# Moving a large SBUF buffer by 384 bytes: a DMA-bound two-pass kernel with its rows 128 bytes past, or on, a multiple of 256

## The chip, the cores and the metric

The kernel runs on one core of a Trainium2 chip. The metric is device time in microseconds (us), the median over several executions. All executions compared below are in the fast state, but for one experiment that was run once and has no state. Ratios are the mean time of one kernel's fast runs over the mean time of the other's fast runs of the same rounds, so they are not quite the ratio of the medians quoted. Readings of packets and spans come from one profiled execution of each kernel, and that one need not lie at the median.

Two words are used throughout. A **packet** is one record of the DMA trace: a contiguous run of bytes that one of the 16 DMA engines moves, with a start, a duration and a size. A start **on 256** is an address that is a multiple of 256 B; one **off 256** is not.

## The reference, cut to what matters

```python
H = W = 384; C = 384                     # x: (1, 384, 384, 384) bf16, 113 MB
g = jnp.einsum("bhwc->bc", x) / (H * W)  # mean of each channel over all pixels
s = _sigmoid(g * w1d[0])                 # k = 1, so the convolution is a product
return x * s[:, None, None, :]           # scale every pixel's channels
```

Every element is needed twice, once for the mean and once for the scaling, and of the 1152 rows that x has in each partition the kernel's buffer in SBUF takes 275. The kernel keeps part of x there (some of it packed, as several fields of bits share words) and reads the rest again: 190 MB are read, of an x of 113.

## The kernel before

All large data lies in one tile, the arena, of 275 rows of C = 384 bf16 values. A row of 384 values is 768 B = 3 x 256 B, so the place of the arena fixes where every row starts relative to 256.

```python
arena = pool.tile([P, ROWS, C], bf16, name="arena")      # ROWS = 275: 211200 B in each partition
ones = pool.tile([P, P], bf16, name="ones")
s_bf = pool.tile([P, C], bf16, name="s_bf")
w_bf = pool.tile([1, 1], bf16, name="w_bf")
...                                                      # zeros, w_sc, seen, worst, odd, odd_i
```

Tiles are placed in the order of these lines, at steps of 32 B. Loads and stores take whole rows of the arena, so that each of the 128 partitions gives one contiguous run on both sides:

```python
def view(t, r0, n):                                      # n rows in each partition, contiguous in HBM
    return t[r0 * P : (r0 + n) * P, :].rearrange("(p r) c -> p r c", r=n)
...
nc.sync.dma_start(out=arena[:, a : a + hi - lo, :], in_=view(xf, r0, n)[:, lo:hi, :])   # load
...
nc.sync.dma_start(out=view(of, r0, n)[:, lo:hi, :], in_=arena[:, a : a + hi - lo, :])   # store
```

Pass one loads everything; TensorE sums rows into PSUM (L226), VectorE and ScalarE pack and check some of them (L250, L256, L290). Pass two scales on VectorE (L432) and stores, and loads again what was not kept. One queue issues all 138 transfers.

Of the kernel before, what the change touches and what calls it, by code (L numbers as in the profile page):

```python
# [127 lines left out]
def kernel(  # L128
# [12 lines left out]
    P = nc.NUM_PARTITIONS  # L141
    B, H, W, C = x.shape
# [5 lines left out]
    bf16, f32, u16, u32 = x.dtype, mybir.dt.float32, mybir.dt.uint16, mybir.dt.uint32  # L148
# [14 lines left out]
    ROWS = base  # L163
# [7 lines left out]
    pool = ctx.enter_context(tc.tile_pool(name="sb", bufs=1))  # L171
    psum = ctx.enter_context(tc.tile_pool(name="psum", bufs=1, space=bass.MemoryType.PSUM))

    pieces = [(g, lo, min(PIECE, q - lo)) for g, q in enumerate(QS) for lo in range(0, q, PIECE)]
    arena = pool.tile([P, ROWS, C], bf16, name="arena")
    ones = pool.tile([P, P], bf16, name="ones")
    s_bf = pool.tile([P, C], bf16, name="s_bf")
    w_bf = pool.tile([1, 1], bf16, name="w_bf")
    zeros = pool.tile([P, P], bf16, name="zeros")
    w_sc = pool.tile([P, 1], f32, name="w_sc")  # L180
    seen = pool.tile([P, 2 * len(pieces)], f32, name="seen")
    worst = pool.tile([P, 1], f32, name="worst")
    odd = pool.tile([P, 1], bf16, name="odd")
    odd_i = pool.tile([P, 1], mybir.dt.int32, name="odd_i")
    bank0 = psum.tile([P, nc.PSUM_BANK_SIZE_BYTES // 4], f32, name="bank0")
    acc, votes = bank0[:, 0:C], bank0[:, C : C + 1]
# [564 lines left out]
```

## Time and profile before

| | before |
|---|---|
| time | 728.79 us, median of 3 (726.57 to 729.08); the profiled execution took 729.99 |
| bytes moved | 303.67 MB by the main queue: 190 MB read from HBM, 113 MB written |
| transfers | 82 loads, 56 stores, 128 data packets each |
| busiest | DMA 98.4%, VectorE 68% |

Two lines of the list of DMA issues (transfers of one size, KB each, median us from issue to landing) and one of the groups by form (busy us, mean ns, idle before):

```profile
arena<-in_x_dram SPq DMA_DIRECT2D x17, 4608.0 KB, 34.8
out_dram<-arena SPq DMA_DIRECT2D x6, 4608.0 KB, 44.4
...
L432 DVE TENSOR_TENSOR arena<-arena,s_bf 128x6144 bf16<-128x6144 bf16 x26 | 85.7, 3351 | 48.2 <-DMA arena<-in_x_dram 48.2
```

4608 KB at the 430 GB/s of the stretches below take 11 us; they land 35 to 44 us after issue, in a queue that is busy for 98.4% of the span, so I take it that others are ahead of them. VectorE's scaling waits for the loads (48.2 us in this group). The prediction below shows the other lines.

### The profile page before, as it was taken

How to read it: one execution, taken by the hardware profiler on the slowest of the kernel's cores; microseconds unless marked ns; L12 is line 12 of the kernel's file. 1: busy time of each engine (PE TensorE's matmuls, PEld its weight loads, DVE VectorE, ACT ScalarE, POOL GpSimd, SP SyncE). 2: the span in 40 equal slices, each digit the busy share in tenths (PEclk: the TensorE clock that was granted, in tenths of full speed). 3: DMA queues.
4: the chain of work that ended last, by engine and by line, in shares of the span. 5: the costliest groups of instructions: out<-in, count | busy, mean ns of one | idle time of the engine just before them, and what ended most of it. 6: DMA issues, size and time to landing. Idle time of an engine off the chain costs nothing.

```text
span 728.2 us, 3243 instructions
## 1 busy us (share of the span) xinstructions
PE 211.9 (29%) x1202; PEld 118.1 (16%) x1202; DVE 496.2 (68%) x469; ACT 115.4 (16%) x92; POOL 0.2 (0%) x4
## 2 busy tenths in 40 slices
PE   4677978889887770000000000000000000000000
PEld 2334535545443430000000000000000000000000
DVE  4600007887985729998999997999969993355330
ACT  3600005665764520001000000000000000000000
POOL 0000000000000000000000000000000000000000
PEclk9899999999999996555555555555555555555555
DMA  9999999999999978999999999999999999999996
GB/s 379 426 433 436 425 419 429 430 430 427 426 422 424 409 315 334 415 420 428 431 415 442 421 428 426 427 442 430 417 425 438 434 434 427 421 433 448 419 430 273
DMA packets 19890, 303.87 MB, mean 417 GB/s; under 512 B 2210, under 2 KB 2210, under 8 KB 6434
## 3 DMA queue, kind: packets, MB, share of 16 engines
q1 hardware_dynamic: 19872, 303.67, 98.4%
q8 instruction: 9, 0.15, 0.1%
q14 instruction: 7, 0.06, 0.0%
q10 hardware_dynamic: 2, 0.00, 0.0%
HBM read 190.41 MB, written 113.25 MB: 417 GB/s over the span
## 4 chain that ended last, share of the span: by engine, by line
DMA 56%; DVE 27%; PE 6%; another core or an unknown queue 4%; ACT 2%; SPq 1%; issue 0%; DVEq 0%
DMA arena<-in_x_dram 41%; DVE arena L432 18%; DMA out_dram<-arena 16%; PE bank L226 6%; DVE arena L250 5%; DVE arena L256 4%; ACT arena L290 2%; SPq L220 1%; ACT s_bf L423 0%; PE bank L504 0%; DVE odd L499 0%; DVE odd_i L508 0%; DVE worst L494 0%; DVEq L112 0%
## 5 line engine op out<-in xcount | busy, mean ns | idle before, releaser
L432 DVE TENSOR_TENSOR arena<-arena,s_bf 128x1536 bf16<-128x1536 bf16 (+8 forms) x102 | 241.8, 2411 | 74.9 <-DMA arena<-in_x_dram 60.8
L250 DVE TENSOR_SCALAR arena<-arena 128x1536 uint16<-128x1536 uint16 (+2 forms) x247 | 145.8, 633 | 116.5 <-DMA arena<-in_x_dram 104.1
L226 PE MATMUL bank<-arena,ones 128*128 128x384 bf16 x1152 | 203.7, 338 | 57.8 <-DMA arena<-in_x_dram 57.8
L226 PEld LDWEIGHTS bank<-arena,ones 128*128 128x128 bf16 x1152 | 113.2, 101 | 148.0 <-DMA arena<-in_x_dram 63.8
L256 DVE TENSOR_TENSOR arena<-arena 128x1536 uint16<-128x1536 uint16 (+2 forms) x114 | 121.0, 1061 | 8.5 <-PE bank L226 6.4
L290 ACT ACTIVATE arena<-arena 128x3072 uint16<-128x3072 uint16 (+1 forms) x38 | 102.5, 2696 | 147.8 <-DVE arena L250 147.8
L360 ACT COPY arena<-bank 128x512 uint32<-128x512 uint32 (+1 forms) x7 | 4.0, 570 | 70.7 <-DMA out_dram<-arena 70.6
L241 PE MATMUL bank<-ones,zeros 128*128 128x384 bf16 x48 | 8.3, 326 | 0.0
L290 ACT ACTIVATION_READ_ACCUMULATOR arena<-arena 128x1 f32 x38 | 7.1, 186 | 0.0
L241 PEld LDWEIGHTS bank<-ones,zeros 128*128 128x128 bf16 x48 | 4.7, 98 | 3.1
L504 PE MATMUL bank<-odd,ones 128*128 128x1 bf16 x1 | 0.2, 186 | 15.8 <-DVE odd L499 15.8
L360 ACT COPY bank<-arena 128x512 uint32<-128x512 uint32 (+1 forms) x7 | 3.6, 566 | 0.0
L504 PEld LDWEIGHTS bank<-odd,ones 128*128 128x128 bf16 x1 | 0.1, 104 | 16.2 <-DVE odd L499 16.2
L423 ACT ACTIVATE s_bf<-bank,w_sc 128x384 bf16<-128x384 f32 x1 | 0.6, 580 | 12.6 <-PE bank L226 12.6
L719 ACT ACT_TABLE_LOAD x1 | 1.3, 1283 | 0.7 <-PEq L735 0.7
L320 DVE TENSOR_SCALAR w_sc<-bank 128x1 f32<-128x1 f32 x1 | 0.2, 159 | 1.4 <-PE bank L315 1.4
L315 PE MATMUL bank<-w_bf,ones 1*128 1x1 bf16 x1 | 0.2, 182 | 2.4 <-DMA w_bf<-in_w1d_dram 2.4
L310 DVE MEMSET ones<- 128x128 bf16 x1 | 0.2, 165 | 1.0 <-SPq L106 1.0
L315 PEld LDWEIGHTS bank<-w_bf,ones 1*128 1x128 bf16 x1 | 0.1, 100 | 2.4 <-DMA w_bf<-in_w1d_dram 2.4
L508 DVE CAST odd_i<-bank 128x1 int32<-128x1 f32 x1 | 0.2, 159 | 0.3 <-PE bank L504 0.3
L494 DVE TENSOR_REDUCE worst<-seen 128x1 f32<-128x38 f32 x1 | 0.2, 182 | 0.0
L499 DVE TENSOR_SCALAR odd<-worst 128x1 bf16<-128x1 f32 x1 | 0.2, 156 | 0.0
(5 smaller groups left out, 0.5 us busy)
## 6 DMA issues: line engine op xcount, KB each, us to landing
arena<-in_x_dram SPq DMA_DIRECT2D x17, 4608.0 KB, 34.8
out_dram<-arena SPq DMA_DIRECT2D x6, 4608.0 KB, 44.4
arena<-in_x_dram SPq DMA_DIRECT2D x21, 1248.0 KB, 11.7
arena<-in_x_dram SPq DMA_DIRECT2D x9, 2304.0 KB, 27.5
out_dram<-arena SPq DMA_DIRECT2D x8, 2304.0 KB, 29.4
arena<-in_x_dram SPq DMA_DIRECT2D x4, 4512.0 KB, 34.8
out_dram<-arena SPq DMA_DIRECT2D x3, 4512.0 KB, 27.0
out_dram<-arena SPq DMA_DIRECT2D x9, 1248.0 KB, 12.1
```

The costliest lines, as they stand in the source:

```text
L220: lambda: nc.sync.dma_start(out=arena[:, a : a + hi - lo, :], in_=view(xf, r0, n)[:, lo:hi, :]),
L226: return nc.tensor.matmul(acc, lhsT=ones[:], rhs=arena[:, i, :], start=first, stop=last)
L241: lambda: nc.tensor.matmul(acc, lhsT=zeros[:], rhs=ones[:, None, :].to_broadcast([P, C // P, P]), start=False, stop=False),
L250: lambda: nc.vector.tensor_scalar(out=dst, in0=src, scalar1=s0, scalar2=s1, op0=op0, op1=op1),
L256: "DVE", lambda: nc.vector.tensor_tensor(out=dst, in0=a, in1=b, op=op), reads=reads, writes=writes
L290: lambda: nc.scalar.activation(out=y, in_=y, func=ACTF.Copy, accum_out=seen[:, 2 * k + i : 2 * k + i + 1]),
L315: lambda: nc.tensor.matmul(votes, lhsT=ones[0:1, :], rhs=w_bf[0:1, 0:1], start=True, stop=True),
L360: "ACT", lambda: nc.scalar.copy(dst.bitcast(u32), src.bitcast(u32)), reads=reads, writes=writes
L423: lambda: nc.scalar.activation(out=s_bf[:], in_=acc, func=ACTF.Sigmoid, scale=w_sc[:, 0:1]),
L432: lambda: nc.vector.tensor_tensor(out=v, in0=v, in1=s_bf[:, None, :].to_broadcast([P, n, C]), op=Op.mult),
L504: lambda: nc.tensor.matmul(votes, lhsT=ones[:], rhs=odd[:], start=True, stop=True),
L719: nc.scalar.preload_act_table(ACTF.Sigmoid)
```

## The change

The intent is that every row in SBUF starts on 256. Five small tiles go ahead of the arena; they take up 384 B. Nothing else is touched.

```diff
-    arena = pool.tile([P, ROWS, C], bf16, name="arena")
+
     ones = pool.tile([P, P], bf16, name="ones")
-    s_bf = pool.tile([P, C], bf16, name="s_bf")
     w_bf = pool.tile([1, 1], bf16, name="w_bf")
-    zeros = pool.tile([P, P], bf16, name="zeros")
     w_sc = pool.tile([P, 1], f32, name="w_sc")
-    seen = pool.tile([P, 2 * len(pieces)], f32, name="seen")
     worst = pool.tile([P, 1], f32, name="worst")
     odd = pool.tile([P, 1], bf16, name="odd")
+    arena = pool.tile([P, ROWS, C], bf16, name="arena")
+    s_bf = pool.tile([P, C], bf16, name="s_bf")
+    zeros = pool.tile([P, P], bf16, name="zeros")
+    seen = pool.tile([P, 2 * len(pieces)], f32, name="seen")
     odd_i = pool.tile([P, 1], mybir.dt.int32, name="odd_i")
```

## The prediction

> **What bounds the kernel now.** I read the activity slices of the page first, then its queue table, then the busy time by stretches, then the waits, then the single packet records of the trace. The slices and queues:
>
> ```profile
> DVE  4600007887985729998999997999969993355330
> DMA  9999999999999978999999999999999999999996
> GB/s 379 426 433 436 425 419 429 430 430 427 426 422 424 409 315 334 415 420 428 431 415 442 421 428 426 427 442 430 417 425 438 434 434 427 421 433 448 419 430 273
> DMA packets 19890, 303.87 MB, mean 417 GB/s; under 512 B 2210, under 2 KB 2210, under 8 KB 6434
> ...
> q1 hardware_dynamic: 19872, 303.67, 98.4%
> ```
>
> The DMA row is at 9 nearly everywhere; the exceptions are slices 15 and 16 (255 to 291 us, where the column sum ends, the sigmoid runs and the first rows are scaled) and the last one. Queue 1 keeps the 16 DMA engines busy 98.4% of the span, so any gain has to come out of the engine time of the transfers or out of the small remainder. The stretches say how fast the engines go while they are busy, and which engine would be next:
>
> ```profile
> core 0: us, PE busy (x) PEld busy (x) DVE busy (x) ACT busy (x) POOL busy (x), PEclk, DMA share, GB/s
> ...
> 60.00:120.00 60.00, 49.38 (x280) 28.12 (x280) 6.78 (x10) 4.95 (x3) 0.00 (x0) 0.94 1.00 430
> ...
> 272.00:300.00 28.00, 0.19 (x1) 0.10 (x1) 27.03 (x24) 0.55 (x1) 0.00 (x0) 0.59 0.89 349
> 300.00:400.00 100.00, 0.00 (x0) 0.00 (x0) 95.73 (x87) 3.99 (x7) 0.00 (x0) 0.50 1.01 425
> 400.00:500.00 100.00, 0.00 (x0) 0.00 (x0) 94.70 (x73) 0.00 (x0) 0.00 (x0) 0.50 1.01 429
> ...
> 600.00:700.00 100.00, 0.00 (x0) 0.00 (x0) 46.65 (x16) 0.00 (x0) 0.00 (x0) 0.50 1.00 430
> 700.00:728.20 28.20, 0.00 (x0) 0.00 (x0) 0.00 (x0) 0.00 (x0) 0.00 (x0) 0.50 0.76 327
> ```
>
> With the DMA share at 1.00 the kernel moves 425 to 430 GB/s, whether it only loads (60 to 120 us) or loads and stores (400 to 700 us). VectorE is the second limit: 94.70 of 100 us busy between 400 and 500, so about 5% of room there, more elsewhere. Last, the waits:
>
> ```profile
> DVE arena L250 <- DMA arena<-in_x_dram: 104.1, 12, 78.2
> ...
> PEld bank L226 <- DMA arena<-in_x_dram: 63.8, 35, 7.3
> DVE arena L432 <- DMA arena<-in_x_dram: 60.8, 9, 20.4
> PE bank L226 <- DMA arena<-in_x_dram: 57.8, 36, 7.5
> ```
>
> PE and VectorE wait for loads; the DMA seldom waits for them. The bound is the engine time of the packets.
>
> Each of the 138 transfers that queue 1 makes (82 loads, 56 stores) shows as 128 data packets, one for each partition and as long as that transfer's rows in it, and 16 packets of 4 B that report the end: 138 x 144 = 19872, the count in the table. The records give a duration for each packet. Most common values, in ns, beside the bytes at 27.2 B/ns (the slope between 4608 B and 36864 B: 32256 B in 1186 ns):
>
> ```
> bytes   count  most common  bytes/27.2  over
>  3072     512      121        112.9      8.1
>  9984    3840      375        367.1      7.9
> 18432    2176      686        677.6      8.4
> 36864    2944     1364       1355.3      8.7
>     4    2208        9          0.1      8.9
> ```
>
> So a data packet costs its bytes at 27.2 B/ns, plus about 8.3 ns, whatever its size. Loads alone (before 260 us) and stores alone (after 700 us) have the same commonest value: 1364 ns for 36864 B in both. Per engine the span is made of: 303.67 MB / 16 / 27.2 = 697.8 us of bytes; 17664 / 16 = 1104 data packets x 8.3 ns = 9.2 us; 138 reports x 9 ns = 1.2 us; some 8.3 us by which packets ran longer than that rule (716.4 us of packet time in all, less the three sums); and 728.2 - 716.4 = 11.8 us idle (2.0 us before the first packet, 2.2 us after the last, most of the rest around 270 to 280 us).
>
> [...]
>
> **The change part by part.** The built program places the arena at byte 16512 of each partition before, 64 x 256 + 128, and at 16896 = 66 x 256 after. A row of 384 bf16 values has 768 B = 3 x 256, so before every row starts 128 B past a boundary of 256 and after every row starts on one. Nothing is added or removed: on every engine the two programs have the same instructions in the same order (PE 12 merged rows in both, VectorE 303, ScalarE 24, GpSimd 69, the issuing queue 116), apart from shifted line numbers. Semaphores and buffers stay.
>
> - DMA, per byte: nothing to gain. [...]
> - Longer packets: some of the 8.3 us could go if the offset causes them. They lie mostly where loads run alone and near 272 to 300 us, and rarely in the mixed stretch, at the same offset. I count 0 to 1 us.
> - VectorE: the scaling takes 3351 ns for 6144 elements and 1749 for 3072, 1.92 elements per ns; the bit operations 960 ns for 3072 and 554 for 1536, 3.78 per ns. One is half the other per element, and both grow linearly in size, so I see no per-row penalty to remove. 0 us. PE reads rows in 326 ns at the minimum, which is also its median, and waits for loads; 0 us.
> - What passes to the end: the DMA is the bound in most stretches and VectorE has 4 to 5% of room in the tightest, so a saving of 0.7% in engine time passes nearly whole.
>
> The sum is 0 if the 8.3 ns are a fixed price, 2.1 us if only reads pay, 5.2 us if both sides do: at most 0.7% of 728.8, far inside 2%.
>
> **The rivals.**
> First, no effect: the time stays at 728 to 729 us. For it: loads and stores cost the same 8.3 ns, though in a load it is memory that is read, in rows that are whole multiples of 768 B, and in a store it is SBUF. A rule for reads alone would make the two differ, unless something else fills the gap. And the 4 B reports, which [...]have nothing to do with the arena, last 9 ns[...]. Both speak for a price per packet that knows nothing of alignment.[...] I give it 65%.
> Second, both sides pay: about 723.5 us. For it: equal cost of loads and stores[...]. Against: the reports. 20%.
> Third, reads alone pay: 726.5 us. Against it: the equal cost. 10%.
> Fourth, the last 5%: the move changes something unseen, such as the longer packets of the first 260 us, where a better placement might give 2 to 4 us more; or VectorE, fed a little faster between 300 and 600 us, takes the bound and part of a DMA gain is lost[...].[...]
>
> **Range and chances.** The weighted mean is 0.65 x 728.5 + 0.20 x 723.5 + 0.10 x 726.5 + 0.05 x 726 = 727.2; as the most likely case lies above it, I say 727.5. The three runs of before spread from 726.6 to 729.1 already, so the upper end is 730 and the lower end 722.5, just under the second rival. Faster by over 2% means under 714.2 us, 14.6 us to be saved: more than the whole price of the packets, 9.2 us. I give it 0.02. Slower by over 2% needs 14.6 us of new work where none is added: 0.01.
>
> **What would show it right or wrong.** In the packet records: 36864 B still at 1364 ns in loads and in stores (no effect)[...]. The queue's share of busy time should stay near 98.4% and the stretch from 600 to 700 us at 430 GB/s, against 431 to 432 if packets shrink. Packet counts, the 138 transfers and the VectorE durations should not change. The prediction is wrong if [...]the time per byte changes, if 18432 B loads lose their scatter above 686 ns, or if VectorE's 3351 ns moves.

Where the marks stand, passages are cut that rest on a price per packet which no trace or run of this case shows: how the fixed 8.3 ns might be made up, why nothing was to be gained per byte, the terms of the sum for stores and for loads, part of the case for the first two rivals, and some of the signs to look for. The sum came to 0 us if the 8.3 ns are a fixed price, 2.1 us if only reads pay and 5.2 us (0.7% of the time) if both sides do. The terms behind the 2.1 and 5.2 us are those cut, and the rivals at 726.5 and 723.5 us and the low end of the range stand on them; what is left of the sum is 0 per byte, for VectorE and for PE, and 0 to 1 us for longer packets.

## The result, and the profile after

The changed kernel takes **722.32 us** (median of 4, 721.76 to 722.96), the kernel before beside it 728.62 us (median of 4). The ratio is 0.9919, with a 95% interval of 0.9898 to 0.994. That is 0.8% faster: clear of noise, and inside 2%.

The page of the changed kernel, the lines that answer to those of before (lines of the source are one higher, L432 is now L433):

```profile
span 721.2 us, 3243 instructions
...
DMA  9999999999999988999999999999999999999997
GB/s 386 426 429 430 444 414 428 432 431 430 427 428 426 418 342 320 408 424 430 432 430 439 424 436 432 427 446 428 428 433 431 441 431 435 422 439 428 438 436 323
DMA packets 19890, 303.87 MB, mean 421 GB/s; under 512 B 2210, under 2 KB 2210, under 8 KB 6434
...
q1 hardware_dynamic: 19872, 303.67, 98.7%
```

The same packets and bytes went 7.0 us sooner (span 728.2 to 721.2), at 421 instead of 417 GB/s. The profiled executions (729.99 and 722.96 us) are slower than their medians, so this difference is somewhat more than the 6.3 us between the medians. The busy time by stretches:

```profile
60.00:120.00 60.00, 50.18 (x275) 28.25 (x276) 6.09 (x9) 4.22 (x3) 0.00 (x0) 0.91 1.00 431
...
300.00:400.00 100.00, 0.00 (x0) 0.00 (x0) 96.62 (x89) 4.00 (x7) 0.00 (x0) 0.50 1.01 429
400.00:500.00 100.00, 0.00 (x0) 0.00 (x0) 96.04 (x77) 0.00 (x0) 0.00 (x0) 0.50 1.01 433
...
600.00:700.00 100.00, 0.00 (x0) 0.00 (x0) 43.11 (x14) 0.00 (x0) 0.00 (x0) 0.50 1.00 433
700.00:721.20 21.20, 0.00 (x0) 0.00 (x0) 0.00 (x0) 0.00 (x0) 0.00 (x0) 0.50 0.79 342
```

The last number of a line is GB/s, the one before it the DMA share. At the same share of 1.00 to 1.01 the rate went from 425 to 429 (300 to 400 us), from 429 to 433 and from 430 to 433. VectorE (the third pair of numbers) is busy for 96.04 of 100 us, so it comes nearer to being the bound but does not become it. The compute itself is unchanged, and what waits for loads waits a little less:

```profile
L433 DVE TENSOR_TENSOR arena<-arena,s_bf 128x6144 bf16<-128x6144 bf16 x26 | 85.7, 3351 | 46.1 <-DMA arena<-in_x_dram 46.1
...
DVE arena L251 <- DMA arena<-in_x_dram: 100.8, 11, 77.8
...
DVE arena L433 <- DMA arena<-in_x_dram: 57.5, 9, 20.2
PE bank L227 <- DMA arena<-in_x_dram: 54.9, 33, 7.2
```

**Where the time came from** is in the packet records. With loads and stores taken together, the commonest duration of every size is what it was: 36864 B take 1364 ns, 18432 B 686, 9984 B 375, 4 B 9, so the price of 8.3 ns on a packet did not move. What moved are the packets that run *longer* than that. I take the excess of each packet over the commonest duration of its size, sum it, and divide by 16 for one engine:

| stretch, us | before, us per engine | after |
|---|---|---|
| 0 to 60, loads | 0.84 | 0.65 |
| 60 to 250, loads | 1.55 | 0.68 |
| 250 to 300, end of the sum, first stores | 2.51 | 2.15 |
| 300 to 700, loads and stores | 3.46 | 0.43 |
| all | 8.36 | 3.90 |

Two different things shrank. From 60 to 250 us 3836 of some 5046 packets ran up to 12 ns long before (1.18 us of the 1.55); after, 17 did. From 300 to 700 us few packets ran long, but by much: 206 by more than 50 ns before (3.36 us), 29 after (0.42 us). Given to loads and stores in the order of the program, 190 of the 206 and 27 of the 29 were loads.

The first of the two is not a price that every load packet pays. By slices of 10 us, packets at most 20 ns over the commonest exceed their bytes (at 27.2 B/ns) in the kernel before by 8.5 ns from 10 to 20 us, as after the change (8.4); by 9.5 from 30 to 40; and by about 12 only from 50 us on, where after the change it stays between 8.0 and 9.5 up to 250 us. From 300 us on, where loads and stores alternate, ordinary load packets (at most 50 ns too long) stand at 8.61 ns before and 8.24 after. The 4 ns belong to long runs of loads alone.

The end of the program shows what this does to the total. The last transfer reports its end 16 times, once for each engine. The mean of these reports moved from 722.27 to 717.70 us, 4.57 us sooner, which agrees with the 4.45 us by which the summed packet time of an engine fell (716.40 to 711.95). But the last of the 16 moved from 726.29 to 719.26, 7.03 us sooner: the engines had drifted 5.68 us apart before and 2.58 us after, and the end waits for the slowest. So 4.57 us are shorter packets on the average engine, and 7.03 - 4.57 = 2.46 us are engines that end closer together.

The second number has the same source as the first. The records can be sorted into 16 sequences, one for each engine, since each packet starts just before the one ahead of it ends (99% of them fit so), mostly by 3 to 4 ns; of the 8.2 ns on a packet some 4 to 5 then keep the engine from the next one. From 300 us on the sum by which an engine's packets exceed their bytes plus 8.2 ns each is 2.1 to 7.2 us before, with a median of 2.5, and 0.0 to 1.6 us after, with a median of 0.2. That sum and the time at which the engine ends go together (correlation 0.98 before, 0.93 after): the long packets fall mostly on a few engines, and the program ends with the one that got most of them.

### The profile page after: what moved, and what is told of

Read it like the earlier page. It is cut to its first block, busy times and chain, and to the rows that moved or that the text cites. A ratio compares the mean times of both kernels' runs of the same rounds, so it can differ in the third digit from the quotient of the medians.

```text
span 721.2 us, 3243 instructions
## 1 busy us (share of the span) xinstructions
PE 213.6 (30%) x1202; PEld 118.9 (16%) x1202; DVE 496.2 (69%) x469; ACT 115.4 (16%) x92; POOL 0.2 (0%) x4
## 4 chain that ended last, share of the span: by engine, by line
DMA 56%; DVE 27%; PE 6%; another core or an unknown queue 4%; ACT 2%; SPq 1%; issue 0%; DVEq 0%
DMA arena<-in_x_dram 41%; DVE arena L433 18%; DMA out_dram<-arena 15%; DVE arena L251 6%; PE bank L227 6%; DVE arena L257 4%; ACT arena L291 2%; SPq L221 1%; ACT s_bf L424 0%; PE bank L505 0%; DVE odd L500 0%; DVE odd_i L509 0%; DVE worst L495 0%; DVEq L112 0%
## 5 line engine op out<-in xcount | busy, mean ns | idle before, releaser
L433 DVE TENSOR_TENSOR arena<-arena,s_bf 128x1536 bf16<-128x1536 bf16 (+8 forms) x102 | 241.8, 2411 | 71.8 <-DMA arena<-in_x_dram 57.5
```

Source lines behind the costliest of these rows:

```text
L433: lambda: nc.vector.tensor_tensor(out=v, in0=v, in1=s_bf[:, None, :].to_broadcast([P, n, C]), op=Op.mult),
```

## The experiments

The theories: **A**, the start of the arena's rows relative to 256 lengthens the packets of loads, which write there. Its rivals: **B**, the small tiles' own new places; **C**, chance. Within A, the question is whether the transfers do it by themselves (A1) or only against compute (A2), which side of a transfer counts, and what the long packets from 300 us on are.

One table has the readings of all but one run. "Loads alone" is the mean time by which packets between 60 and 250 us exceed their bytes at 27.2 B/ns (those at most 20 ns over the commonest). "Long" counts packets over 50 ns too long between 300 and 700 us. "Spread" is the time between the first and last of the last transfer's 16 reports. The runs come from different chips; the kernel before had a median of 728.2 to 728.9 us.

| run | SBUF start, mod 256 | median us | loads alone, ns | long: count, us per engine | spread, us |
|---|---|---|---|---|---|
| before | 128 | 728.62 | 12.05 | 206, 3.36 | 5.68 |
| after | 0 | 722.32 | 8.26 | 29, 0.42 | 2.58 |
| rest_aligned | 128 | 729.90 | 12.08 | 147, 2.82 | 6.87 |
| arena_only | 0 | 722.96 | 8.22 | 28, 0.37 | 2.32 |
| off64 | 64 | 729.82 | 12.22 | 113, 2.41 | 5.60 |
| off32 | 32 | 730.08 | 13.22 | 148, 3.03 | 6.14 |
| dma_off128 | 128 | 721.94 | 12.11 | 106, 1.95 | 6.09 |
| dma_off0 | 0 | 715.27 | 8.22 | 15, 0.34 | 2.87 |
| dram128_sb0 | 0 | 716.57 | 8.25 | 29, 0.62 | 3.33 |
| dram128_sb128 | 128 | 720.06 | 12.19 | 28, 0.54 | 3.64 |
| l0_s0 | loads 0, stores 0 | 715.51 | 8.22 | 33, 0.61 | 4.06 |
| l0_s128 | loads 0, stores 128 | 714.26 | 8.23 | 60, 0.95 | 4.34 |
| l128_s0 | loads 128, stores 0 | 715.80 | 12.19 | 22, 0.27 | 3.41 |

### Which tile counts

**rest_aligned** leaves the arena at byte 16512, 128 off, and brings ones, s_bf and zeros onto 256:

```diff
     arena = pool.tile([P, ROWS, C], bf16, name="arena")
+    # w_bf, w_sc, worst, odd now stand here (4 x 32 B), then:
     ones = pool.tile([P, P], bf16, name="ones")
     s_bf = pool.tile([P, C], bf16, name="s_bf")
```

> Arena left 128 B past a multiple of 256 as in the kernel before, but ones, s_bf and zeros moved to multiples of 256. Theory A (the start of the arena rows, as the place that loads write to, lengthens load packets): nothing gained, 728 to 729 us; in the packet records loads before 250 us keep their scatter of 4 to 8 ns over the commonest value, and load packets over 50 ns too long stay near 250 after 300 us's neighbourhood (180 or so from 300 to 700 us). Theory B (the small tiles' own placement makes the gain): 722 to 723 us. Theory C (chance of the run or of the chip): no rule, anything from 721 to 729.

**arena_only** puts the arena at 16640 = 65 x 256, and leaves ones, s_bf and zeros 32 B off:

```diff
+    # w_bf, w_sc, worst, odd stand here (4 x 32 B), then:
     arena = pool.tile([P, ROWS, C], bf16, name="arena")
+    # then odd_i (32 B), ones, s_bf, zeros, seen
```

> Arena at a multiple of 256 (16640, another one than the change's 16896), but ones, s_bf and zeros left 32 B past one. Theory A: the whole gain, 721.5 to 723 us, few long load packets between 300 and 700 us (under 40). Theory B: none, 728 to 729 us.

Against the kernel before in the same rounds (728.42 us), rest_aligned has the ratio 1.0011 (0.9992 to 1.0029) and arena_only 0.9928 (0.9914 to 0.9942). B falls: with the small tiles moved alone nothing is gained. C falls too: two aligned layouts and two at 128 give the same two times, and nearly the same packet readings (rest_aligned has 147 long packets, where some 180 had been expected). The rates by slices of the two, rest_aligned first:

```profile
GB/s 381 424 433 436 425 420 428 429 430 428 424 425 421 410 315 333 417 427 425 431 426 441 412 434 417 439 438 434 414 433 430 427 448 415 426 435 439 429 436 255
```

```profile
GB/s 383 428 426 431 444 414 431 430 433 426 431 427 428 419 346 322 409 425 428 434 428 439 425 437 429 431 439 437 429 432 433 437 429 429 432 433 442 432 430 329
```

The last slice tells the spread: 255 GB/s where the engines end far apart, as in the kernel before (273), and 329 where they end together, as after (323).

### Transfers without compute

**dma_off128** and **dma_off0** are the kernels before and after with all compute left out. Their outputs are wrong, which doesn't matter for the times.

```diff
     def add(self, eng, emit, reads=(), writes=(), dma=False, after=()):
+        if eng != "SP":
+            return None
```

> All work of the compute engines taken out (wrong result on purpose), the transfers left, arena 128 B off as before. Some 707 to 718 us, as bytes alone are 698 us and packets' fixed price adds some 5 to 10 us. If the offset lengthens load packets by itself (A1), this is 4 to 7 us slower than the same with the arena on a multiple of 256, with scattered load packets. If it does so only against the compute engines' accesses to SBUF (A2), both take the same within 1 us and no load packet scatters.

> The same transfers alone, arena on a multiple of 256. A1: 4 to 7 us faster than with the arena 128 B off. A2: equal within 1 us.

721.94 against 715.27 us: 6.7 us, as much as in the full kernel. A1 holds and A2 falls: no compute engine is needed for the loss, and since no VectorE or TensorE instruction is left, no speed of theirs is needed for a gain of this size. Both times lie at or above the upper part of what I had expected for the bare transfers (707 to 718). Stretches of dma_off128, then of dma_off0:

```profile
60.00:250.00 190.00, 0.00 (x0) 0.00 (x0) 1.00 1.00 427
...
500.00:600.00 100.00, 0.00 (x0) 0.00 (x0) 1.00 1.00 429
```

```profile
60.00:250.00 190.00, 0.00 (x0) 0.00 (x0) 1.00 1.01 431
...
500.00:600.00 100.00, 0.00 (x0) 0.00 (x0) 1.00 1.00 432
```

With loads alone the rate is 427 against 431 GB/s, with loads and stores 429 against 432 in this stretch (400 to 500 us likewise; from 300 to 400 both have 432, from 600 to 700 it is 432 against 434).

### Other offsets

**off64** and **off32** put 192 B and 160 B of small tiles ahead of the arena, so that it starts at 16704 (64 past a multiple) and 16672 (32 past):

```diff
+    # w_bf, w_sc, worst, odd, odd_i stand here (off32), and a pad of 32 B (off64)
     arena = pool.tile([P, ROWS, C], bf16, name="arena")
```

> The full kernel with the arena 64 B past a multiple of 256. If only a start on a multiple of 256 is free (A), 727 to 731 us, with scattered load packets. If the penalty is that of 128 alone (an odd half of 256), or grows with the offset, it lies between 722.5 and 728. If a multiple of 64 were enough, 128 B would have cost nothing, so that is out already.

> The full kernel with the arena 32 B past a multiple of 256[...]. A with a penalty that does not depend on the offset: 727 to 731 us. A penalty that grows with the bytes below the start: about 724 us.

Both took the loss whole: 729.82 and 730.08 us, ratios 1.0025 (1.0011 to 1.0038) and 1.003 (1.0016 to 1.0045) to the kernel that is 128 off. An offset of 32 B costs no less than one of 128; loads alone cost it even a nanosecond more (13.22 against 12.05). So the loss does not grow with the offset among these three, and 32 or 64 is not enough of an alignment.

### Which side of a transfer

**dram128_sb0** and **dram128_sb128** are the two bare kernels again, but every transfer except that of the very first rows takes its place in HBM 128 B earlier (the store of the first rows leaves a row out, to keep off its neighbour). Where x and out start in HBM the trace does not say; "128 off" is relative to where they are in the runs without a shift. That the unshifted ones lie on 256 is not shown, so for HBM only the effect of a shift by 128 B is.

```diff
     def view(t, r0, n):
-        return t[r0 * P : (r0 + n) * P, :].rearrange("(p r) c -> p r c", r=n)
+        lo = r0 * P * C - (64 if r0 else 0)             # 64 elements = 128 B earlier
+        return (xl if t is xf else ol)[lo : lo + n * P * C].rearrange("(p r c) -> p r c", r=n, c=C)
```

> Transfers alone (wrong result on purpose), arena on a multiple of 256, but every transfer but those of the first rows reads x and writes out 128 B earlier, so the HBM side starts 128 B off. Theory D (only the start of the SBUF side of a load counts): 714.5 to 716.5 us, clean load packets, as with the arena at a multiple of 256 and nothing shifted (715.27). Theory E (source and destination must lie alike within 256): about 722 us, scattered loads. Theory F (any write off 256, to HBM too): stores' packets scatter here, over 718 us.

> The same, with the arena 128 B off as well, so both sides are off alike. D: 721 to 723 us (721.94 with the arena alone off). E: about 715 us, clean. F: slower than 722 us.

For loads alone the packets answer: reading HBM 128 off into rows on 256 costs 8.25 ns over the bytes, as unshifted (8.22), and reading it 128 off into rows that are off alike costs 12.19. Only where the load *writes* counts, and a source that lies alike does not help; for this part E falls. For stores, I took the packets between 300 and 700 us, the long ones left out: 8.23 ns over the bytes in dma_off0, 8.23 also in dma_off128, where they read SBUF 128 off, but 12.39 in dram128_sb0, where they write HBM 128 off. So it is not SBUF either, but the place of the write, at about 4 ns (12.39 less 8.23) for a packet on average; here F was right, though the time of over 718 us that it was to have did not come. By the time, dram128_sb0 is 1.3 us slower than dma_off0 (roughly). It was run at another time.

dram128_sb128 has a surprise: off on every side, it took 720.06 us, and hardly any long packets (28), while dma_off128, off in SBUF alone, has 106. No theory had that.

### What the long packets are

**switches** is a kernel of bare transfers written anew for this question, of four phases in one program:

```python
def phase(number, off, pattern):         # 8 loads, then `pattern`; 1.57 MB a transfer, 12288 B a packet
    ...                                  # slot k: arena[:, off + (k % 16) * E : ... + E], off in elements
phase(0, 0, "LS" * 18); phase(1, 64, "LS" * 18)
phase(2, 64, "LLLSSS" * 6); phase(3, 0, "LLLSSS" * 6)
```

> No compute, other transfers (wrong result on purpose): four phases of 8 loads and then 18 loads and 18 stores of 1.57 MB (packets of 12288 B), each phase behind the end of the last. Phase 1: SBUF side on a multiple of 256, load and store in turn (18 changes from load to store). Phase 2: the same 128 B off. Phase 3: 128 B off, three loads, three stores in turn (6 changes). Phase 4: the same on a multiple of 256. The 18 loads are 144 packets an engine. Theory G (a load whose packets start off 256 leaves a delay that comes out at each change from load to store): load packets' excess is some 1.5 us an engine in phase 2, a third of it in phase 3, near 0.1 in 1 and 4, and most of it on the last packet before a store. Theory H (each load packet pays by itself): phases 2 and 3 alike, spread over all load packets; 144 x 4 ns = 0.6 us.

In the mixed part of the four phases, packets over 50 ns too long cost 1.10, 1.95, 0.84 and 0.64 us per engine. The order of 128-off phases fits G (1.95 with 18 changes, 0.84 with 6), but 1.10 and 0.64 on 256, where I had expected 0.1, do not: long packets come without any offset too, and the offset adds 0.85 and 0.20 to them. Sorted into each engine's sequence (over 99% of the records follow their predecessor without a gap), nearly all the excess lies in loads that a store follows: in phase 3 (counted from 1: 128 off, three loads in turn), 0.82 us in the 6 such loads, 0.13 us in the 12 that another load follows. There they are not mainly the last packet before the store, as G had it (0.12 of the 0.82), but the last but one (0.42). In the kernels of the question the place is nearer to G's. Of the 190 long load packets of the kernel before, 182 lie in loads that a store follows, 103 are the last of the eight packets that an engine moves for its load, and 43 the last but one; in dma_off128 it is all 104, with 68 and 21. So G has the place about right, but not the offset as the only source; H, which would have phases 2 and 3 alike, is not right.

**l0_s0**, **l0_s128** and **l128_s0** separate loads from stores in the bare kernels. Each store moves 128 B less in each partition and starts at the row or 128 B into it:

```diff
-  out=view(of, r0, n)[:, lo:hi, :],                        in_=arena[:, a : a + hi - lo, :]
+  out=<the same rows, flat>[:, lo * C : hi * C - 64],      in_=<arena, flat>[:, a * C + START : (a + hi - lo) * C - 64 + START]
   # START, arena at mod 256:  l0_s0: 0, 0    l0_s128: 64, 0    l128_s0: 64, 128
```

> Transfers alone, wrong result on purpose, each store 128 B a partition shorter in all three kernels of this call. Loads write from a multiple of 256, stores read from one. The base of the three: 7040 packets and more, 128 B shorter, are some 2 us less, so 712.5 to 715 us.

> Loads write from a multiple of 256, stores read from 128 B past one. If only the start of a write counts: within 1 us of the base.[...]

> Loads write from 128 B past a multiple of 256, stores read from one. If the loads' writes carry the whole cost: 5 to 7 us slower than the base, with scattered load packets, long load packets after 300 us and a spread of the engines' last reports of over 4 us. If part of it comes from the stores, 2 to 4 us.

Stores that read off 256 cost nothing that the times show (714.26 against 715.51 us; they were even the fastest). But loads that write off 256, alone, cost only 0.3 us by the medians, not 5 to 7: they have their 12.19 ns while they run alone, but few long packets (22) and a spread of 3.41 us. By the profiled executions it is 1.8 us (716.03 against 714.21, the slowest of four against the fastest of four), and the summed packet time of an engine is 2.24 us longer (711.12 against 708.88). My expectation failed, and with it the notion that the loads' writes alone make the whole loss. The runs have a flaw: l0_s0 moves 0.92 MB less than dma_off0, some 2 us at the rate of the others, and takes as long, 715.51 us where 712.5 to 715 had been expected. Its summed packet time did fall by 1.83 us (710.71 to 708.88), but its engines ended further apart (4.06 against 2.87 us). Whether that comes from the shortened stores, which end 128 off in HBM, or from chance in one profiled execution of each is not shown.

So the long packets stand like this: many (106 to 206) in all five runs where loads write and stores read off 256 in SBUF while the HBM side is left as it is; few (15 to 60) in the eight others. In two of the eight, dram128_sb128 and l128_s0, loads write off 256 as well; there the ordinary load packets from 300 to 700 us are longer instead, 10.91 and 10.55 ns over their bytes, against 8.61 in the kernel before and 8.43 in dma_off128. So the loss shows either as a few ns on many packets or as a few long packets, and with long ones more was lost (dma_off128: 721.94 us, with its engines 6.09 us apart at the end; dram128_sb128, in another call: 720.06 and 3.64). What decides between the two, and what joins the two sides, is **open**.

## Why the prediction was right or wrong

The time of 722.32 us lies 0.2 us under the low end of the range (722.5 to 730.0); with the ratio 0.9919 applied to 728.79 us it is 722.9, just inside. "Within 2%" was right. The middle, 727.5, was 5 us too high, because the rival that got 65% was wrong. That the range reached down so far was luck: its low end stood for another mechanism, both sides paying a price that no trace of the kernel before had shown.

- *What bounds the kernel*: right. Bare transfers alone take 715 to 722 us, and with a rate that is 1% higher the program ends 1% sooner. VectorE's room (94.70 to 96.04 of 100 us busy) sufficed, and its 3351 ns did not move.
- *Per byte nothing to gain*: right. Where loads run alone off 256 (60 to 250 us of dma_off128), the commonest durations are 1368, 691 and 380 ns for 36864, 18432 and 9984 B, on 256 1364, 686 and 375: 4 to 5 ns more, whatever the size.
- *"Loads and stores cost the same 8.3 ns"*: this is the step that failed. I compared the commonest durations of all loads before 260 us. 1364 ns leads there for 36864 B, but with only 502 of 1408 packets, mostly of the first 60 us; from 60 to 250 us 1368 ns leads, with 252 of 878. The mean too would have shown the difference in the trace of before: 12.05 ns over the bytes for loads alone from 60 to 250 us, 8.26 ns for stores from 300 us on. The 4 ns between them went in every aligned layout (8.22 to 8.26 ns). The prediction had named the sign itself: it would be wrong if loads of 18432 B lost their scatter above 686 ns. They did: from 60 to 250 us 167 of 1024 took 686 ns before, 1018 of 1024 after. It also means that the fixed price is all of the 8.2 ns, in aligned loads and in stores alike, and the penalty comes on top.
- *Reads pay*: wrong, shown by the stores of dma_off128 (8.23 ns, reading off 256) and by l0_s128 (no slower than l0_s0). *Writes pay*: right in that loads that write off 256 pay, 3.8 ns a packet while they run alone, though it comes as scatter on top of the fixed price and not out of it. All 656 load packets of an engine (82 x 128 / 16) x 3.8 ns would be 2.5 us, but the loads of the first 50 us and those between stores show little of it; what it cost from 60 to 250 us is 1.18 us.
- *"Longer packets ... I count 0 to 1 us"*: the term that was mis-sized. It measured 4.46 us (8.36 to 3.90), of which 3.03 us come from the mixed stretch of 300 to 700 us, where I saw the long packets as rare and took them for something else, "at the same offset". Rare packets carry much: 206 of them cost 3.36 us.
- *Not in the sum at all*: the engines' drift. I divided by 16 and so took all engines as equal. The end waits for the slowest, and 2.46 us of the gain are the smaller spread: the same long packets, unevenly shared out.
- *Second rival, "both sides pay: about 723.5"*: nearest in time, but for other reasons. Its sign, a shorter commonest packet, did not come; for 36864 B it stayed at 1364 ns.

That the start of the arena decides is shown by rest_aligned and arena_only; that the DMA loses by itself, by the bare kernels; that rows that a load writes off 256 lengthen its packets by some 4 ns in long runs of loads (12.19 against 8.25), and that stores are lengthened as much when their place in HBM is moved by 128 B (12.39 against 8.23), by the kernels with the HBM side moved. That the drift is the long packets falling on few engines is shown by the sorted records (correlation 0.98 before, 0.93 after). How an offset makes the long load packets, which with the drift are most of the gain, is open.

## What to carry to other kernels

In a kernel that the DMA bounds, try starting large SBUF buffers on 256 B; here it cost nothing but the order of declarations, and offsets of 32, 64 and 128 B were equally bad here (730.08, 729.82 and 728.62 us, against 722.32 on 256), at 0.8 to 1% of the time. When packet durations are read for such a question, compare means and tails by kind of transfer, not the commonest value (here 1364 ns before and after, while the mean over the bytes went from 12.05 to 8.26 ns where loads run alone); and when many engines share a load, look at when the slowest of them ends, not at the mean (here 7.03 us sooner against 4.57).
